# Second MLP product by Strassen's scheme, with sums of its left factor on VectorE, in a fused Mamba-2 and MLP kernel

## Chip, cores, metric

One core of a Trainium2 chip. The metric is device time of one execution in microseconds (us), median of several runs. All times are of fast runs (runs of one kernel agree within 0.8%); where a single run stands alone its state is unknown, and that is said.

## The reference

A Mamba-2 (SSD) attention block feeds an MLP with a hard-swish. All is fp32.

```python
x = attn(x, a, B, C)            # (4, 8, 768, 32) -> bridged to (3072, 256)
h = x @ w_in                    # (3072, 256) @ (256, 2048)
g = h * clip(h + 3, 0, 6) / 6
out = g @ w_out                 # (3072, 2048) @ (2048, 256)
```

## The kernel before

The tokens are worked in six blocks `k` of 512 (128 positions of four sequences). In each block TensorE first makes the 16 pieces of g (`mlp_in`, the "first product"), then the output (`mlp_out`, the "second product"). The attention steps of the next block are woven in: two of them in the first product (after pieces 9 and 13), five between parts of the second.

```python
def mlp_in(k, f):                       # piece f of 16; gT[:, f] is 128 x 512
    h = ps.tile([P, TB], FP32, name="h", tag="f")          # four buffers in PSUM, shared with "cb"
    for j in range(NK):
        nc.tensor.matmul(out=h, lhsT=w_in[:, j, f*P:(f+1)*P], rhs=yTs[k][:, j]..., ...)
    r = ffn.tile([P, TB], FP32, name="r", bufs=3)
    nc.scalar.activation(r, h, AF.Relu, bias=half, scale=1.0 / 6.0)
    nc.vector.scalar_tensor_tensor(out=gTs[k][:, f], in0=r, scalar=1.0, in1=h, op0=ALU.min, op1=ALU.mult)

def mlp_out(k, b, f0, f1):              # 128 tokens of sequence b, all 256 columns
    for f in range(f0, f1):
        nc.tensor.matmul(out=o, lhsT=gTs[k][:, f, b*P:(b+1)*P], rhs=w_out[:, f], ...)
    ...                                 # ScalarE copies o to SBUF, then a DMA

def decay(c, b):                        # GpSimd prepares the decay rows, ScalarE the exponential
    if c > 1:
        nc.gpsimd.tensor_tensor(out=L, in0=L, in1=by_j, op=ALU.add)          # L252
    nc.gpsimd.affine_select(out=L, in_=L, ...)                               # L253
    if c > 1:
        nc.scalar.activation(L, L, AF.Exp)
    ...
```

Of the kernel before, what the change touches and what calls it, by code (L numbers as in the profile page):

```python
# [1 line left out]

# [6 lines left out]
FP32 = mybir.dt.float32  # L9
# [4 lines left out]
ALU = mybir.AluOpType  # L14
# [5 lines left out]
def kernel(  # L20
# [23 lines left out]
    nc = tc.nc  # L44
    P = 128
    NB, NH, S, D = x.shape
# [4 lines left out]
    NF = DF // P  # L51
# [7 lines left out]
    const = ctx.enter_context(tc.tile_pool(name="const", bufs=1))  # L59
    loads = ctx.enter_context(tc.tile_pool(name="loads", bufs=2))  # L60
    att = ctx.enter_context(tc.tile_pool(name="att", bufs=2))
    ffn = ctx.enter_context(tc.tile_pool(name="ffn", bufs=1))
    ps = ctx.enter_context(tc.tile_pool(name="ps", bufs=4, space=PSUM))
    ps_o = ctx.enter_context(tc.tile_pool(name="ps_o", bufs=2, space=PSUM))
# [30 lines left out]
    w_out = const.tile([P, NF, DM], FP32, name="w_out")  # L95
    NP = 4
    FP = NF // NP
    NRAW = 3
    raws = {}

    def load_w(i):
# [31 lines left out]
        out=head, in_=head, pattern=[[-N * HU, 2], [-N, HU], [0, D]], compare_op=ALU.is_ge,  # L133
        fill=0.0, base=0, channel_multiplier=1)
    nc.gpsimd.affine_select(
        out=head, in_=head, pattern=[[N * HU, 2], [N, HU], [0, D]], compare_op=ALU.is_ge,
# [3 lines left out]
    def decode(i):  # L140
# [43 lines left out]
        out=a_sb, in0=a_sb, scalar1=1e-6, scalar2=1.0, op0=ALU.max, op1=ALU.min)  # L184
    nc.scalar.activation(a_sb, a_sb, AF.Ln)
    nc.vector.tensor_tensor_scan(
        out=flat, data0=run.rearrange("g c p -> g (c p)"), data1=a_sb, initial=0.0,
# [6 lines left out]
    def load_decay(c, b):  # L194
        L = big([P, NH, P], "L")
        src = cum_d[c, b * NH:(b + 1) * NH].rearrange("h p -> (h p)").unsqueeze(0)
        nc.sync.dma_start(
            out=L.rearrange("j h i -> j (h i)"), in_=src.to_broadcast([P, NH * P]))
        Ls[c, b] = L

    def load_eto(c):
        eto = att.tile([P, NB, P], FP32, name="eto")
        for h in range(NH):
            nc.sync.dma_start(  # L204
                out=eto[h * N:(h + 1) * N],
                in_=cum_d[c, h:NB * NH:NH].unsqueeze(0).to_broadcast([N, NB, P]))
        etos[c] = eto
# [19 lines left out]
    for t in range(2):  # L227
        nc.gpsimd.tensor_tensor(
            out=parity[:, t:t + 1], in0=mask[:, t, 0:1], in1=mask[:, 2 + t, 0:1], op=ALU.add)
# [17 lines left out]
    def decay(c, b):  # L247

        L = Ls[c, b]
        if c > 1:  # L250
            by_j = cum_n[:, c, b * NH:(b + 1) * NH].unsqueeze(2).to_broadcast([P, NH, P])
            nc.gpsimd.tensor_tensor(out=L, in0=L, in1=by_j, op=ALU.add)  # L252
        nc.gpsimd.affine_select(  # L253
            out=L, in_=L, pattern=[[0, NH], [1, P]], compare_op=ALU.is_ge,
            fill=-1e5, base=0, channel_multiplier=-1)
        if c > 1:
            nc.scalar.activation(L, L, AF.Exp)  # L257
        else:
            decay_exp(c, b, L, 0, NH)

    def ends(c):


        bc, xt = loaded[c]
        if c < NC - 1:
            bs = att.tile([P, NB * NH, N], FP32, name="bs")
            nc.gpsimd.tensor_tensor(  # L267
                out=bs, in0=bc[:, 1],
                in1=e_from[:, c].unsqueeze(2).to_broadcast([P, NB * NH, N]), op=ALU.mult)
            bss[c] = bs  # L270
        if c:
            eto = etos[c]
            nc.scalar.activation(eto, eto, AF.Exp)  # L273
            if c < NC - 1:
                tmp = att.tile([P, NB, P], FP32, name="tmp", bufs=1)
                nc.gpsimd.tensor_tensor(  # L276
                    out=tmp, in0=states[c - 1],
                    in1=eto[:, :, P - 1:P].to_broadcast([P, NB, P]), op=ALU.mult)
                tmps[c] = tmp

    def turn(c, p):


        bc, xt = loaded[c]
        t_ps = ps_o.tile([P, 4, P], FP32, name="t_ps", tag="o")
        for k in range(4):
            j, b = k // 2, 2 * p + k % 2
            nc.tensor.transpose(
                out=t_ps[:, k],
                in_=bc[:, j, b * NH:(b + 1) * NH].rearrange("s h n -> s (h n)"), identity=ident)  # L290
        bT = att.tile([P, 2, P], FP32, name="bT")
        nc.scalar.copy(out=bT, in_=t_ps[:, 2:4])
        cT = att.tile([P, 2, 2, P], FP32, name="cT")
        nc.vector.tensor_tensor(  # L294
            out=cT, in0=t_ps[:, 0:2].unsqueeze(2).to_broadcast([P, 2, 2, P]),
            in1=parity.unsqueeze(1).unsqueeze(3).to_broadcast([P, 2, 2, P]), op=ALU.mult)
        csT = None
        if c:
            csT = att.tile([P, 2, P], FP32, name="csT")
            nc.vector.tensor_tensor(  # L300
                out=csT, in0=t_ps[:, 0:2], in1=etos[c][:, 2 * p:2 * p + 2], op=ALU.mult)
        bTs[c, p] = bT, cT, csT

    def scores(c, b):
        bT, cT, csT = bTs[c, b // 2]
        cbs = []
        for q in range(NQ):
            rows = slice(32 * q, 32 * q + 32)
            if c == 0 and b % 2 and q < 2:
                cb = ps_o.tile([P, 2, P], FP32, name="cb", tag="o")  # L310
            else:
                cb = ps.tile([P, 2, P], FP32, name="cb", tag="f")
            nc.tensor.matmul(  # L313
                out=cb.rearrange("j h i -> j (h i)"), lhsT=bT[rows, b % 2],
                rhs=cT[rows, b % 2].rearrange("n t i -> n (t i)"), start=True, stop=True,
                tile_position=(32 * q, 0))
            cbs.append(cb)
        L = Ls[c, b]
        for q in range(NQ):
            hs = slice(2 * q, 2 * q + 2)  # L320
            nc.vector.tensor_tensor(out=L[:, hs], in0=L[:, hs], in1=cbs[q], op=ALU.mult)  # L321
# [52 lines left out]
    gTs, outs = {}, {}  # L374
# [15 lines left out]
    def mlp_out(k, b, f0, f1):  # L390
        if f0 == 0:
            outs[k, b] = ps_o.tile([P, DM], FP32, name="o", tag="o")
        o = outs[k, b]
        for f in range(f0, f1):
            nc.tensor.matmul(  # L395
                out=o, lhsT=gTs[k][:, f, b * P:(b + 1) * P], rhs=w_out[:, f],
                start=(f == 0), stop=(f == NF - 1))
        if f1 == NF:
            ob = ffn.tile([P, DM], FP32, name="ob", bufs=3)
            nc.scalar.copy(out=ob, in_=o)  # L400
            r0 = b * S + k * P
            nc.sync.dma_start(out=out[r0:r0 + P, :], in_=ob)

    def steps(c):

        ends(c)
        turn(c, 0)
        decay(c, 0)
        yield
        turn(c, 1)  # L410
        decay(c, 1)
        yield
        for b in range(NB):
            scores(c, b)
            if c + 1 < NC:
                load_decay(c + 1, b)
            if b + 2 < NB:
                decay(c, b + 2)
            if b:
                mix(c, b - 1)  # L420
            if b == 2:
                keep(c, 0)
            yield
        mix(c, 3)
        keep(c, 1)
        if 0 < c < NC - 1:
            load_eto(c + 1)

    def load(c):
        load_bc(c)  # L430
        load_x(c)
# [3 lines left out]
    def weights(i, n):  # L435
        for _ in range(n):
            next(parts[i], None)
# [7 lines left out]
    for i, _ in enumerate(steps(0)):  # L445
        if i > 3:
            weights(1, 1)
# [4 lines left out]
    for i in range(2, NP + 1):  # L452
        for j in range(4):
            weave[4 * i - 7 + j] = i
    for k in range(NC):
        todo = steps(k + 1) if k + 1 < NC else iter(())
        for f in range(NF):
            mlp_in(k, f)
            if k == 0 and f in weave:
                weights(weave[f], 1)  # L460
            if f in (9, 13):
                next(todo, None)
        if k + 2 < NC:
            load(k + 2)
        if k == 0:
            weights(NP + 1, 2)
        if k == 0:
            next(todo, None)
            for i in range(NP):
                for b in range(2):  # L470
                    mlp_out(0, b, i * FP, (i + 1) * FP)
                if i + 1 < NP:
                    weights(NP + i + 1, 2)
                    if i + 2 < NP:
                        weights(NP + i + 2, 2)
                    next(todo, None)
            mlp_out(k, 2, 0, NF)
        else:
            mlp_out(k, 0, 0, NF // 4)
            next(todo, None)  # L480
            mlp_out(k, 0, NF // 4, NF)
            next(todo, None)
            mlp_out(k, 1, 0, NF)
            next(todo, None)
            mlp_out(k, 2, 0, NF // 4)
            next(todo, None)
            mlp_out(k, 2, NF // 4, NF)
        next(todo, None)
        mlp_out(k, 3, 0, NF)


# [28 lines left out]
```

## Time and profile before

| | before |
|---|---|
| time | 432.24 us (432.01 to 432.57) |
| TensorE busy | 404.8 of 430.9 us |
| a middle block (1, 2, 3) | 65.4 us |
| of it first product with two attention steps | 28.7 us |
| of it second product with five | 36.7 us |

A block is counted from the start of its first product to the start of the next block's. TensorE is busy almost without a gap, so what counts is how long its work takes and whether it has to wait.

### The profile page before, as it was taken

To read this page: it belongs to the slowest core of one execution; us is meant where nothing else is said; L and a number is where in the kernel's file an instruction comes from. 1 tells how busy PE (TensorE), PEld (TensorE's weight loads), DVE (VectorE), ACT (ScalarE), POOL (GpSimd) and SP (SyncE) were. 2 spreads that over 40 slices of the span, in tenths; PEclk is the share of its full clock that TensorE was granted. 3 is DMA by queue.
4 is the path that set the end of the run, shared out by engine and by line. 5 is a ranking of instruction groups with operands and counts; after the bars stand their busy time and mean duration, and the time that the engine had idled before them with its cause. 6 is when DMAs were issued, how large, how long until landed. Compare 5 with 4: busy or idle time off the path is not lost.

```text
span 430.9 us, 4977 instructions
## 1 busy us (share of the span) xinstructions
PE 404.8 (94%) x1948; PEld 257.0 (60%) x1948; DVE 158.0 (37%) x289; ACT 148.9 (35%) x268; POOL 70.3 (16%) x61
## 2 busy tenths in 40 slices
PE   1579976999999999999999999999999999999996
PEld 1344432778644777644677744677744677644885
DVE  5656678960134322134322143422134421043100
ACT  5585668931145300135311134310145311134100
POOL 2500060100007500007500006825000000000000
PEclk9998988899999999999999999999999999999999
DMA  8998925911460032370023370023100000000000
GB/s 161 252 314 136 351 97 128 204 60 44 64 112 0 2 99 90 59 121 2 0 75 110 61 124 0 2 71 101 49 2 1 0 25 14 14 0 0 14 12 24
DMA packets 87607, 32.23 MB, mean 75 GB/s; under 512 B 75584, under 2 KB 81408, under 8 KB 87584
## 3 DMA queue, kind: packets, MB, share of 16 engines
q1 hardware_dynamic: 87584, 31.92, 30.4%
q8 instruction: 15, 0.25, 0.2%
q14 instruction: 8, 0.07, 0.0%
HBM read 28.67 MB, written 3.24 MB: 74 GB/s over the span
## 4 chain that ended last, share of the span: by engine, by line
PE 65%; issue 15%; SPq 6%; POOL 4%; DMA 3%; ACT 3%; DVE 2%; POOLq 0%; ACTq 0%
PE o L395 37%; PE h L381 19%; PE cb L313 3%; SPq L204 3%; PE y L342 2%; SPq L84 2%; DMA bc<-in_B_dram 2%; PE y L336 2%; POOL L L253 2%; ACT L L219 1%; DMA eto<-cum_d 1%; POOL L L252 1%; DVE gT L387 1%; PE y L348 1%; ACT r L386 1%
## 5 line engine op out<-in xcount | busy, mean ns | idle before, releaser
L381 PE MATMUL h<-yT,w_in 128*128 128x512 f32 x384 | 172.0, 603 | 6.3 <-DVE w_in L176 2.6
L395 PE MATMUL o<-w_out,gT 128*128 128x256 f32 x768 | 175.9, 387 | 0.0
L395 PEld LDWEIGHTS o<-w_out,gT 128*128 128x128 f32 x768 | 145.7, 192 | 27.0 <-issue 7.2
L381 PEld LDWEIGHTS h<-yT,w_in 128*128 128x128 f32 x384 | 72.9, 193 | 95.0 <-issue 80.3
L387 DVE SCALAR_TENSOR_TENSOR gT<-r,h 128x512 f32<-128x512 f32 x96 | 65.0, 685 | 134.4 <-ACT r L386 134.0
L386 ACT ACTIVATE r<-h,half 128x512 f32<-128x512 f32 x96 | 64.2, 686 | 70.1 <-PE h L381 70.1
L400 ACT COPY ob<-o 128x256 f32<-128x256 f32 x24 | 8.9, 373 | 162.6 <-PE o L395 129.7
L321 DVE TENSOR_TENSOR L<-L,cb 128x256 f32<-128x256 f32 x96 | 33.8, 415 | 61.3 <-PE cb L313 61.3
L276 POOL TENSOR_TENSOR tmp<-state,eto 128x512 f32<-128x512 f32 x4 | 4.2, 1048 | 173.7 <-ACT eto L273 173.7
L252 POOL TENSOR_TENSOR L<-L,cum_n 128x1024 f32<-128x1024 f32 x16 | 30.4, 1897 | 13.0 <-DMA L<-cum_d 13.0
L313 PE MATMUL cb<-cT,bT 32*128 32x256 f32 x192 | 23.2, 477 | 7.4 <-DVE cT L294 5.2
L253 POOL TENSOR_SCALAR_AFFINE_SELECT L<-L 128x1024 f32<-128x1024 f32 x24 | 27.5, 1152 | 4.4 <-DMA L<-cum_d 3.1
L219 ACT ACTIVATE L<-L,cum_n 128x128 f32<-128x128 f32 x64 | 19.3, 389 | 7.2 <-POOL L L253 7.2
L313 PEld LDWEIGHTS cb<-cT,bT 32*128 32x128 f32 x192 | 10.7, 205 | 17.6 <-DVE cT L294 6.3
L257 ACT ACTIVATE L<-L 128x1024 f32<-128x1024 f32 x16 | 17.0, 1063 | 11.8 <-POOL L L253 11.8
L366 DVE TENSOR_TENSOR state<-y,mask 128x256 f32<-128x256 f32 x10 | 4.2, 425 | 37.6 <-ACT yT L363 37.6
L342 PE MATMUL y<-L,xt 128*32 128x128 f32 x384 | 16.9, 296 | 0.1
L158 ACT ACTIVATE we<-we,bias_hi 128x1024 bf16<-128x1024 uint16 x8 | 9.2, 1148 | 11.0 <-DVE we L156 11.0
L342 PEld LDWEIGHTS y<-L,xt 128*32 128x32 f32 x384 | 9.9, 115 | 4.8 <-issue 2.1
L267 POOL TENSOR_TENSOR bs<-bc,e_from 128x512 f32<-128x512 f32 x5 | 5.9, 1188 | 38.3 <-DMA bc<-in_B_dram 30.5
L363 ACT COPY yT<-y 128x256 f32<-128x256 f32 x24 | 7.7, 373 | 10.7 <-PE y L348 9.2
L336 PEld LDWEIGHTS y<-csT,state 64*128 64x128 f32 x80 | 6.0, 184 | 6.6 <-issue 6.6
(46 smaller groups left out, 132.9 us busy)
## 6 DMA issues: line engine op xcount, KB each, us to landing
L<-cum_d SPq DMA_DIRECT2D x24, 512.0 KB, 5.0
raw<-in_moe_w_in_dram SPq DMA_DIRECT2D x4, 1024.0 KB, 8.4
raw<-in_moe_w_out_dram SPq DMA_DIRECT2D x4, 1024.0 KB, 6.5
xt<-in_x_dram SPq DMA_DIRECT2D x6, 512.0 KB, 6.9
out_dram<-ob SPq DMA_DIRECT2D x24, 128.0 KB, 1.7
bc<-in_C_dram SPq DMA_DIRECT2D x6, 256.0 KB, 5.7
bc<-in_B_dram SPq DMA_DIRECT2D x6, 256.0 KB, 7.6
eto<-cum_d SPq DMA_DIRECT2D x40, 32.0 KB, 1.9
```

Of the source, the lines that this page charges most:

```text
L219: nc.scalar.activation(Ls[c, b][:, h0 + q], src[:, q], AF.Exp, bias=cum_n[:, c, g:g + 1])
L252: nc.gpsimd.tensor_tensor(out=L, in0=L, in1=by_j, op=ALU.add)
L253: nc.gpsimd.affine_select(out=L, in_=L, pattern=[[0, NH], [1, P]], compare_op=ALU.is_ge, fill=-1e5, base=0, channel_multiplier=-1)
L257: nc.scalar.activation(L, L, AF.Exp)
L313: nc.tensor.matmul(out=cb.rearrange("j h i -> j (h i)"), lhsT=bT[rows, b % 2], rhs=cT[rows, b % 2].rearrange("n t i -> n (t i)"), start=Tr ...
L321: nc.vector.tensor_tensor(out=L[:, hs], in0=L[:, hs], in1=cbs[q], op=ALU.mult)
L336: nc.tensor.matmul(out=y_ps[u][:, k], lhsT=states[c - 1][rows, b], rhs=csT[rows, k], start=True, stop=False, skip_group_check=True)
L342: nc.tensor.matmul(out=y_ps[u][32 * q:32 * q + 32, k], lhsT=xt[:, b * NH + h], rhs=L[:, h], start=(c == 0), stop=True, tile_position=(0, 3 ...
L381: nc.tensor.matmul(out=h, lhsT=w_in[:, j, f * P:(f + 1) * P], rhs=yTs[k][:, j].rearrange("p b i -> p (b i)"), start=(j == 0), stop=(j == N ...
L386: nc.scalar.activation(r, h, AF.Relu, bias=half, scale=1.0 / 6.0)
L387: nc.vector.scalar_tensor_tensor(out=gTs[k][:, f], in0=r, scalar=1.0, in1=h, op0=ALU.min, op1=ALU.mult)
L395: nc.tensor.matmul(out=o, lhsT=gTs[k][:, f, b * P:(b + 1) * P], rhs=w_out[:, f], start=(f == 0), stop=(f == NF - 1))
```

## The change

The output of a block is a product of a 512 x 2048 by a 2048 x 256 matrix. It is cut into quarters (tokens of sequences 0, 1 and 2, 3; even and odd pieces f; left and right half of the columns). Strassen's scheme in Winograd's form makes seven products of quarters in place of eight, from sums of quarters. Four sums of the weights are made once on GpSimd; four sums of g are made in every block from 1 to 5 on VectorE, for two pairs of pieces at a time, after pieces 3, 7, 11 and 15. A "unit" is one quarter product for 128 tokens: eight matmuls over 128 columns. Its result goes to one of four slots of a PSUM tile, `oa` or `ob`, which the program calls a bank.

```diff
+    def weight_sums():                      # once, on GpSimd: t1 .. t4 from quarters of w_out
+        ...
+    def g_sums(k, j0):
+        js = slice(j0, j0 + 2)
+        a11, a12, a21, a22 = (g_quarter(k, e, r)[:, js] for r in range(2) for e in range(2))
+        s1, s2, s4 = (gsums[k][n][:, js] for n in (1, 2, 4))
+        for o, p_, q_, op in ((s1, a21, a22, ALU.add), (s2, s1, a11, ALU.subtract),
+                              (a21, a11, a21, ALU.subtract), (s4, a12, s2, ALU.subtract)):
+            nc.vector.tensor_tensor(out=o, in0=p_, in1=q_, op=op)
+    def out_units(k, t):                    # t: which 128 tokens of each pair of sequences
+        oa = ps_o.tile([P, 4, P], FP32, name="oa", tag="o")
+        unit(oa, 1, quarter(1, 0), w4[:, 1, 0]);  yield
+        unit(oa, 2, total(2), wsums[2]);          yield
+        unit(oa, 0, quarter(0, 0), w4[:, 0, 0])
+        ...                                 # x1 = oa0 (ScalarE); res0, res4 = oa1, oa2 + x1 (VectorE)
+        yield
+        ob = ps_o.tile([P, 4, P], FP32, name="ob", tag="o")
+        unit(ob, 2, total(4), w4[:, 1, 1]);       yield
+        unit(ob, 3, quarter(1, 1), wsums[4]);     yield
+        unit(ob, 0, total(1), wsums[1]);          yield
+        unit(ob, 1, quarter(0, 1), wsums[3])
+        ...                                 # three VectorE operations, two DMAs
@@ main loop
+            if k and f % 4 == 3:
+                g_sums(k, f // 2 - 1)
@@
-            mlp_out(k, 0, 0, NF // 4)
-            next(todo, None)
-            ...                             # mlp_out of 0, 1, 2, 3 with the attention steps between
+            units = itertools.chain(out_units(k, 0), out_units(k, 1))
+            for i, _ in enumerate(units):
+                if i in (0, 3, 6, 9, 11):
+                    next(todo, None)
```

The intent: TensorE is the bound, and an eighth less of the second product should shorten it, with sums on engines that have time.

More of the change, by code (lines that the diff above doesn't have):

```diff
@@ L1 @@
+import itertools
 from contextlib import ExitStack
@@ L402, in mlp_out @@
             nc.sync.dma_start(out=out[r0:r0 + P, :], in_=ob)
+    NJ = NF // 2
+    w4 = w_out.rearrange("p (j e) (m c) -> p e m j c", e=2, m=2)
+    wsums = {}
+    def weight_sums():
+        t3 = const.tile([P, NJ, P], FP32, name="t3")
+        t2, t4 = (att.tile([P, NJ, P], FP32, name=n, tag="wm") for n in ("t2", "t4"))
+        t1 = w4[:, 0, 1]
+        for o, p_, q_ in ((t3, w4[:, 1, 1], w4[:, 0, 1]), (t1, w4[:, 0, 1], w4[:, 0, 0]),
+                          (t2, w4[:, 1, 1], t1), (t4, w4[:, 1, 0], t2)):
+            nc.gpsimd.tensor_tensor(out=o, in0=p_, in1=q_, op=ALU.subtract)
+        wsums.update({1: t1, 2: t2, 3: t3, 4: t4})
@@ new lines, with g_quarter @@
+    gsums, ends_out = {}, {}
+    def g_quarter(k, e, r):
+        return gTs[k].rearrange("p (j e) (r i) -> p e r j i", e=2, r=2)[:, e, r]
+    def g_sums(k, j0):
+        if j0 == 0:
+            gsums[k] = {n: loads.tile([P, NJ, 2 * P], FP32, name=f"s{n}", tag="raw", bufs=NRAW)
+                        for n in (1, 2, 4)}
+        js = slice(j0, j0 + 2)
[4 more added lines that the diff above has]
+            nc.vector.tensor_tensor(out=o, in0=p_, in1=q_, op=op)
@@ new lines, in out_units, with quarter, total, unit @@
+    def out_units(k, t):
+        def quarter(e, r):
+            return g_quarter(k, e, r)[:, :, t * P:(t + 1) * P]
+        def total(n):
+            return gsums[k][n][:, :, t * P:(t + 1) * P]
+        def unit(bank, slot, lhs, rhs):
+            for j in range(NJ):
+                nc.tensor.matmul(
+                    out=bank[:, slot], lhsT=lhs[:, j], rhs=rhs[:, j],
+                    start=(j == 0), stop=(j == NJ - 1), skip_group_check=True)
+        oa = ps_o.tile([P, 4, P], FP32, name="oa", tag="o")
+        unit(oa, 1, quarter(1, 0), w4[:, 1, 0])
+        yield
+        unit(oa, 2, total(2), wsums[2])
+        yield
+        unit(oa, 0, quarter(0, 0), w4[:, 0, 0])
+        x1 = ffn.tile([P, P], FP32, name="x1", bufs=2)
+        nc.scalar.copy(out=x1, in_=oa[:, 0])
+        res = ffn.tile([P, 5, P], FP32, name="res", bufs=2)
+        nc.vector.tensor_tensor(
+            out=res[:, 0:5:4], in0=oa[:, 1:3], in1=x1.unsqueeze(1).to_broadcast([P, 2, P]),
+            op=ALU.add)
+        yield
+        ob = ps_o.tile([P, 4, P], FP32, name="ob", tag="o")
+        unit(ob, 2, total(4), w4[:, 1, 1])
+        yield
+        unit(ob, 3, quarter(1, 1), wsums[4])
+        yield
+        unit(ob, 0, total(1), wsums[1])
+        yield
+        unit(ob, 1, quarter(0, 1), wsums[3])
+        u = ffn.tile([P, 2, P], FP32, name="u", bufs=2)
+        nc.vector.tensor_tensor(
+            out=u, in0=ob[:, 0:2], in1=res[:, 4:5].to_broadcast([P, 2, P]), op=ALU.add)
+        nc.vector.tensor_tensor(out=res[:, 1:3], in0=ob[:, 2:4], in1=u, op=ALU.add)
+        nc.vector.tensor_tensor(out=res[:, 3], in0=ob[:, 0], in1=u[:, 1], op=ALU.add)
+        for r in range(2):
+            r0 = (t + 2 * r) * S + k * P
+            nc.sync.dma_start(
+                out=out[r0:r0 + P, :], in_=res[:, 2 * r:2 * r + 2].rearrange("p m c -> p (m c)"))
+        yield
@@ L477 @@
             mlp_out(k, 2, 0, NF)
-        else:
-            mlp_out(k, 0, 0, NF // 4)
-            next(todo, None)
-            mlp_out(k, 0, NF // 4, NF)
-            next(todo, None)
-            mlp_out(k, 1, 0, NF)
-            next(todo, None)
-            mlp_out(k, 2, 0, NF // 4)
-            next(todo, None)
-            mlp_out(k, 2, NF // 4, NF)
-        next(todo, None)
-        mlp_out(k, 3, 0, NF)
+            next(todo, None)
+            mlp_out(k, 3, 0, NF)
+            weight_sums()
+        else:
+            units = itertools.chain(out_units(k, 0), out_units(k, 1))
+            for i, _ in enumerate(units):
+                if i in (0, 3, 6, 9, 11):
+                    next(todo, None)
 _INS = ['x', 'a', 'B', 'C', 'moe_w_in', 'moe_w_out']
```

## The prediction

Statements on the hardware that no trace or run of this case shows are cut from the recorded text below, and from the expectations of x_psum and x_m64; the cuts are marked. No term of the forecast's sum is cut: it came to -16.1 + 0.8 + 18.8 + 0.6 + 5.1 = +9.2, and with the lean to the longer wait to 442.0 us. What stands behind the terms in the trace of the kernel before:

- *Pace*: the 0.109 us an instruction is that of the four transposes (0.44 us from 326.25).
- *Turns*: the view from 11.60 us shows GpSimd and VectorE side by side; "these" are its two operations. The overlap of 0.14 us is worked out from it: L165 ends at 13.75, less its own 0.685 that is 13.07, while GpSimd's operation is stamped to 13.21. The turns at 56 us are L176 from 56.18 (1.98 us, 1.22 alone) and L253 from 57.03 (2.08, 1.09 alone). L294, with its 685 ns, has 512 columns; the 0.60 is from its start at 205.04 to that of L300 at 205.64.
- *Clock*: the two stretches of the view lie around a wait of TensorE from 55.97 to 58.21. The term is an estimate: one stretch of 3.42 us at half clock, as shown there, for each of the three stalls, half of it lost.
- *Other estimates*: an addition over 128 columns at 0.3 us (425 ns for 256 columns in L366, 685 for 512 in L294); the 0.3 for blocks 4 and 5, the 0.3 for block 3 and the 0.14 of R3 are not measured.

> **What bounds the kernel now.** I read the page's busy shares and groups first, then the chain of waits, then the timelines of GpSimd and VectorE in one block. The page:
>
> ```profile
> PE 404.8 (94%) x1948; PEld 257.0 (60%) x1948; DVE 158.0 (37%) x289; ACT 148.9 (35%) x268; POOL 70.3 (16%) x61
> ...
> L395 PE MATMUL o<-w_out,gT 128*128 128x256 f32 x768 | 175.9, 387 | 0.0
> L395 PEld LDWEIGHTS o<-w_out,gT 128*128 128x128 f32 x768 | 145.7, 192 | 27.0 <-issue 7.2
> ```
>
> TensorE is the bound. The program has 384 second-product matmuls and the trace 768: each fp32 product is two instructions, each with its weight load. The chain gives their pace, in the last block and around four 128-column transposes:
>
> ```profile
> 326.25 0.44 PE t_ps L288 x4
> ...
> 372.60 27.47 PE h L381 x64
> 400.07 27.64 PE o L395 x128
> ...
> 427.78 0.37 ACT ob L400
> ```
>
> 27.47 us / 64 = 0.429 us for 512 columns, 27.64 / 128 = 0.216 for 256, 0.44 / 4 = 0.11 for 128. Pace follows the moving columns, although one weight load is stamped 192 ns. A middle block (178.2 to 243.5 us) takes 65.3 us, of which TensorE is idle some 0.1. On its way the other engines do this:
>
> ```profile
> 199.85 1.09 POOL L253 TENSOR_SCALAR_AFFINE_SELECT L<-L 128x1024 f32<-128x1024 f32 x1
> 200.92 1.90 POOL L252 TENSOR_TENSOR L<-L,cum_n 128x1024 f32<-128x1024 f32 x1
> 202.89 1.09 POOL L253 TENSOR_SCALAR_AFFINE_SELECT L<-L 128x1024 f32<-128x1024 f32 x1
> 203.95 1.90 POOL L252 TENSOR_TENSOR L<-L,cum_n 128x1024 f32<-128x1024 f32 x1
> 205.92 1.09 POOL L253 TENSOR_SCALAR_AFFINE_SELECT L<-L 128x1024 f32<-128x1024 f32 x1
> 206.99 1.90 POOL L252 TENSOR_TENSOR L<-L,cum_n 128x1024 f32<-128x1024 f32 x1
> 208.96 1.09 POOL L253 TENSOR_SCALAR_AFFINE_SELECT L<-L 128x1024 f32<-128x1024 f32 x1
> ```
> ```profile
> 202.64 2.48 DVE L387 SCALAR_TENSOR_TENSOR gT<-r,h 128x512 f32<-128x512 f32 x4 [4.53 <-ACT r L386]
> 205.04 0.68 DVE L294 TENSOR_TENSOR cT<-t_ps,parity 128x512 f32<-128x512 f32 x1
> 205.64 0.41 DVE L300 TENSOR_TENSOR csT<-t_ps,eto 128x256 f32<-128x256 f32 x1
> 206.18 0.69 DVE L387 SCALAR_TENSOR_TENSOR gT<-r,h 128x512 f32<-128x512 f32 x1
> 207.84 0.69 DVE L387 SCALAR_TENSOR_TENSOR gT<-r,h 128x512 f32<-128x512 f32 x1 [0.98 <-ACT r L386]
> ```
>
> Here GpSimd works without a pause while VectorE makes the last six pieces of g (10 to 15; the four of the first row are 10 to 13). VectorE was held until 202.64 because ScalarE stood at an exponential waiting for GpSimd. Piece 15 is ready at 208.5, just when TensorE, done with the first product at 206.92, needs it: no slack, and no loss yet.
>
> [...]
>
> ```profile
> 11.60 1.61 POOL L267 TENSOR_TENSOR bs<-bc,e_from 128x512 f32<-128x512 f32 x1 [7.79 <-ACT e_from L242]
> 12.20 1.55 DVE L165 TENSOR_TENSOR we<-we,ws 128x1024 uint16<-128x1024 uint16 x1
> ```
>
> Alone these take 1.06 and 0.685 us (medians of their groups). The preceding VectorE operation (two SBUF inputs too) held GpSimd back, then GpSimd held L165 back: they take turns, even when VectorE's next is already queued. [...] L294 of that width shows 685, consecutive independent ones start 0.60 apart. [...] the clock is the third number from the end of a row (1.00, then 0.50):
>
> ```profile
> 55.75:59.16 3.41, 1.16 (x3) 0.49 (x3) 3.41 (x4) 0.48 (x3) 3.13 (x3) 1.00 0.74 284
> 59.16:62.58 3.42, 3.42 (x5) 1.35 (x4) 1.81 (x4) 3.00 (x9) 3.42 (x3) 0.50 0.06 23
> ```
>
> **The change, part by part.** *Matmuls.* Per block 64 products over 256 columns become 2 x 7 x 8 = 112 over 128. As instructions, 128 x 0.216 = 27.6 us become 224 x 0.109 = 24.4 us: 3.2 saved, x 5 blocks = **-16.1 us**. [...] 0.12 instead of 0.109 would cost 2.5 us a block.
>
> *Sums of weights*: four GpSimd operations (about 1.9 us each by L252) after the end of block 0. They end about 6 us into block 1, whose second product starts 28 us in: hidden.
>
> *Evacuation*: per half block three VectorE operations on ob (0.42 + 0.42 + 0.3) for ScalarE's 0.37 copies. Hidden, except behind the very last matmul: **+0.8 us**.
>
> *Sums of g*: four VectorE operations of 512 columns, two SBUF inputs each, after pieces 3, 7, 11 and 15: about 2.7 us each time, 11 us a block; VectorE has 45 us free in 65. After pieces 3 and 7 GpSimd is idle and VectorE catches up within three pieces. **After piece 11 it is not.** In the frame of the block above, piece 11 ends at 203.93; until 210.05 GpSimd has four operations without a gap, and the two engines take turns. Net of the 0.14 overlap: 4 x 0.55 for VectorE and 1.76 + 0.95 + 1.76 + 0.95 for GpSimd, so the sums end at 203.95 + 7.6 = 211.6 instead of 206.6. Behind them, in order, pieces 12, 13, cT, csT, pieces 14, 15 at 0.60, 0.60, 0.60, 0.40, 0.60, then 0.69: piece 15 is ready at 215.1. TensorE finishes the first product at 206.92 as before; the first unit's matmuls alternate two instructions per odd piece, reach piece 13 at 208.2 and piece 15 at 206.92 + 14 x 0.109 = 208.45, and wait until 215.1: **6.7 us**. If VectorE gets the first turn at 203.95 (the two ask within 0.01 us of each other), one GpSimd operation fewer stands ahead: 5.8. I take 6.3. The built program's waits confirm it: the first unit waits for VectorE at exactly two of its eight products, pieces 13 and 15, and for none of the sums.
>
> The same GpSimd run lies at 132 to 145 and 262 to 278 us, so this hits blocks 1, 2 and 3: **+18.8 us**. Blocks 4 and 5 have no GpSimd work there; VectorE's own delay costs some 0.15 each: +0.3. In block 3 GpSimd goes straight on to the next chunk and may hold the sums after piece 15: +0.3.
>
> *Clock*: [...] losing half: 1.7 x 3 = **+5.1 us**.
>
> Sum: -16.1 + 0.8 + 18.8 + 0.6 + 5.1 = +9.2; as the waiting GpSimd operation at 203.95 was queued a hair earlier I lean to the longer wait: 432.3 + 9.7 = **442.0 us**.
>
> **Rivals.** *R1, no contention that matters*: [...] my alignment is off by some us. For it: the sums are short, and catching up on paper leaves 0.7 us at piece 15. Against: the turns shown at 11.6 us and again at 56 us. Then -16.1 + 0.8 + 0.8 = 418. *R2, contention but no half clock, first turn to VectorE*: 3 x 5.8 - 15 = 434 to 435. *R3, weight loads become the bound*: 128-column loads of full fp32 weights behind 128-column matmuls stand in the trace only as transposes and in half-height pairs. For it: the stamp of 192 ns[...]. At 0.14 per instruction the matmuls lose instead of gain: 31.4 a block, 477 with the stalls. Against: after a change of shape two loads of L395 start 0.11 apart.
>
> **Range and chances.** The terms of the middle are the gain (certain within 2 us), three stalls (5.5 to 7 each)[...]: 434 to 448. R1 and R3 widen the tails: 433 to 450. A result under 423.8 needs R1 (7%); over 440.9 is just below my centre (55%); between, 38%.
>
> **What would show it.** Right: units of L449 at 0.109 us an instruction, 24.4 us of such work a block; the sums (L437) at some 0.7 us in blocks 4 and 5 and after pieces 3, 7 and 15, but 1.7 to 2.6 after piece 11 in blocks 1 to 3, with L252 and L253 there stretched by some 0.5; TensorE idle about 6 us at the start of each of those second products, released by VectorE's gT (L388); a clock of 0.50 just behind; blocks 1 to 3 longer than 65.3 by 3 to 6 us, block 5 shorter by 3. Wrong: sums that run straight through, or a pace of 0.12 and more in a block without waits.

## The result, and the profile after

The change makes the kernel slower: **446.66 us** (445.9 to 446.77, 4 runs) against 432.24, a ratio of 1.033 (95% interval 1.031 to 1.035). A ratio is the mean of one kernel's fast runs over that of the other's fast runs of the same rounds, so it is not quite the ratio of the medians. Line numbers are shifted by one in the changed kernel (L387 is now L388, L252 and L253 are L253 and L254); the units are L449 and the sums of g L437.

From the page of the changed kernel: busy shares, granted clock in 40 slices (tenths of full speed), and the costliest group of the units:

```profile
PE 399.5 (90%) x2428; PEld 269.5 (61%) x2428; DVE 237.3 (53%) x409; ACT 144.0 (32%) x258; POOL 84.5 (19%) x65
...
PEclk9999987999999699999889999969999999999999
...
L449 PE MATMUL oa<-w_out,gT 128*128 128x128 f32 x320 | 42.4, 282 | 18.4 <-DVE gT L388 18.4
```

TensorE has less to do (399.5 for 404.8 us) in a longer span: it waited 18.4 us for VectorE's g, and the clock row has three dips in the middle that the kernel before does not have. In the timelines below, the first two numbers of a line are its start and its length in us, `x12` says that twelve instructions in a row are merged, and the bracket gives the engine's idle time before the line and what ended it. TensorE in block 2, at the start of the second product:

```profile
212.09 1.50 PE L449 MATMUL oa<-w_out,gT 128*128 128x128 f32 x12
218.10 0.49 PE L449 MATMUL oa<-w_out,gT 128*128 128x128 f32 x2 [4.51 <-DVE gT L388]
220.22 0.79 PE L449 MATMUL oa<-w_out,gT 128*128 128x128 f32 x2 [1.64 <-DVE gT L388]
```

The first twelve instructions run; those that need piece 13 wait 4.51 us, those that need piece 15 another 1.64. VectorE in the same stretch (after the two pieces 10 and 11, the four sums, then pieces 12, 13, cT, csT and pieces 14, 15):

```profile
207.81 1.28 DVE L388 SCALAR_TENSOR_TENSOR gT<-r,h 128x512 f32<-128x512 f32 x2 [4.30 <-ACT r L387]
209.12 2.43 DVE L437 TENSOR_TENSOR s<-gT 128x512 f32<-128x512 f32 x1
211.59 1.46 DVE L437 TENSOR_TENSOR s<-s,gT 128x512 f32<-128x512 f32 x1
212.98 2.38 DVE L437 TENSOR_TENSOR gT<-gT 128x512 f32<-128x512 f32 x1
215.28 1.57 DVE L437 TENSOR_TENSOR s<-gT,s 128x512 f32<-128x512 f32 x1
216.77 1.27 DVE L388 SCALAR_TENSOR_TENSOR gT<-r,h 128x512 f32<-128x512 f32 x2
```

and GpSimd:

```profile
209.12 1.90 POOL L253 TENSOR_TENSOR L<-L,cum_n 128x1024 f32<-128x1024 f32 x1
211.09 1.43 POOL L254 TENSOR_SCALAR_AFFINE_SELECT L<-L 128x1024 f32<-128x1024 f32 x1
212.49 2.32 POOL L253 TENSOR_TENSOR L<-L,cum_n 128x1024 f32<-128x1024 f32 x1
214.88 1.43 POOL L254 TENSOR_SCALAR_AFFINE_SELECT L<-L 128x1024 f32<-128x1024 f32 x1
```

Read the two side by side. The first sum is stamped from 209.12 but ends only at 211.55, some 0.5 us after GpSimd's 1.90 us operation (to 211.02); the next GpSimd operation takes 1.43 in place of 1.09, and so on, turn by turn. The four sums take 7.7 us (209.12 to 216.85); away from GpSimd they have a median of 0.68 to 0.69 us each. Last, two stretches of block 2 with the granted clock as third number from the end (before it the busy times of TensorE, its weight loads, VectorE, ScalarE, GpSimd; behind it the DMA share and GB/s):

```profile
210.00:218.48 8.48, 3.97 (x20) 2.50 (x18) 8.45 (x7) 2.24 (x4) 7.62 (x5) 1.00 0.00 0
218.48:225.30 6.82, 5.18 (x26) 4.20 (x26) 5.60 (x12) 0.70 (x1) 0.00 (x0) 0.50 0.01 2
```

The half clock begins while TensorE waits and lasts until 225.30, 5.1 us after the wait is over.

How long the blocks took in each trace, from the start of the first product to the next block's (for block 5: its second product, which no attention step interrupts, from the start of its first instruction to the start of its last):

| run | block 1 | block 2 | block 3 | block 4 | block 5, second product |
|---|---|---|---|---|---|
| before | 65.4 | 65.4 | 65.4 | 63.5 | 27.4 |
| changed | 71.8 | 71.7 | 71.7 | 61.1 | 25.1 |
| x_sums | 74.1 | 74.6 | 74.8 | 63.5 | 27.4 |
| x_nosums | 64.8 | 62.9 | 62.9 | 61.1 | 25.1 |
| x_psum | 64.2 | 64.2 | 65.8 | 61.1 | 25.1 |
| x_fill | 69.4 | 69.4 | 70.5 | 61.1 | 25.1 |
| x_late | 64.4 | 64.4 | 65.9 | 61.7 | 26.5 |
| y_late | 64.2 | 64.2 | 64.7 | 62.4 | 27.7 |
| y_late_noload | 64.2 | 64.2 | 64.2 | 62.4 | 27.7 |
| y_bank | 62.9 | 62.9 | 63.9 | 61.1 | 25.1 |

So the change gains 2.4 us in block 4 and 2.3 in block 5, and loses 6.4 in each of blocks 1 to 3. Block 0, whose code is the same in all, took 78.1 to 80.8 us: an offset of up to some 2.7 us between single traces that the edits do not explain. Part of it is the clock: the two shortest (x_fill, y_late) are the two whose traces have 3.4 us at half clock in block 0, the others have some 10. So effects of a few us are read from the blocks, not from the totals.

### The profile page after: what moved, and what is told of

It is laid out like the page before. It is cut to its first block, busy times and chain, and to the rows that moved or that the text cites. A ratio compares the mean times of both kernels' runs of the same rounds, so it can differ in the third digit from the quotient of the medians.

```text
span 445.0 us, 6046 instructions
## 1 busy us (share of the span) xinstructions
PE 399.5 (90%) x2428; PEld 269.5 (61%) x2428; DVE 237.3 (53%) x409; ACT 144.0 (32%) x258; POOL 84.5 (19%) x65
## 4 chain that ended last, share of the span: by engine, by line
PE 57%; issue 17%; DVE 11%; SPq 4%; POOL 4%; ACT 3%; DMA 2%; POOLq 0%; DVEq 0%; ACTq 0%
PE ob L449 15%; PE h L382 13%; PE oa L449 13%; PE o L396 7%; DVE s L437 4%; PE cb L314 4%; DVE gT L388 3%; PE y L343 3%; SPq L85 2%; DMA bc<-in_B_dram 2%; PE y L337 2%; DVE gT L437 2%; POOL L L254 1%; ACT L L220 1%; PE y L349 1%
## 5 line engine op out<-in xcount | busy, mean ns | idle before, releaser
L388 DVE SCALAR_TENSOR_TENSOR gT<-r,h 128x512 f32<-128x512 f32 x96 | 63.8, 683 | 65.5 <-ACT r L387 65.4
L387 ACT ACTIVATE r<-h,half 128x512 f32<-128x512 f32 x96 | 64.2, 686 | 99.1 <-PE h L382 80.3
L449 PE MATMUL oa<-w_out,gT 128*128 128x128 f32 x320 | 42.4, 282 | 18.4 <-DVE gT L388 18.4
L449 PEld LDWEIGHTS oa<-w_out,gT 128*128 128x128 f32 x320 | 38.9, 194 | 23.0 <-DVE gT L388 19.6
L449 PE MATMUL ob<-w_out,s 128*128 128x128 f32 x320 | 39.8, 278 | 0.0
L449 PE MATMUL ob<-t,gT 128*128 128x128 f32 x320 | 39.4, 276 | 0.0
L449 PEld LDWEIGHTS ob<-w_out,s 128*128 128x128 f32 x320 | 37.3, 192 | 1.4 <-issue 1.4
L449 PEld LDWEIGHTS ob<-t,gT 128*128 128x128 f32 x320 | 37.3, 192 | 0.7 <-issue 0.7
L253 POOL TENSOR_TENSOR L<-L,cum_n 128x1024 f32<-128x1024 f32 x16 | 32.0, 2003 | 19.6 <-DMA L<-cum_d 19.6
L396 PE MATMUL o<-w_out,gT 128*128 128x256 f32 x128 | 31.7, 409 | 0.0
L254 POOL TENSOR_SCALAR_AFFINE_SELECT L<-L 128x1024 f32<-128x1024 f32 x24 | 29.9, 1249 | 5.0 <-DMA L<-cum_d 3.9
L396 PEld LDWEIGHTS o<-w_out,gT 128*128 128x128 f32 x128 | 25.9, 206 | 5.2 <-issue 1.0
L449 PEld LDWEIGHTS oa<-t,s 128*128 128x128 f32 x160 | 23.2, 231 | 2.3 <-issue 2.3
L449 PE MATMUL oa<-t,s 128*128 128x128 f32 x160 | 24.5, 317 | 0.0
```

What stands on the lines that cost most here:

```text
L254: nc.gpsimd.affine_select(out=L, in_=L, pattern=[[0, NH], [1, P]], compare_op=ALU.is_ge, fill=-1e5, base=0, channel_multiplier=-1)
L396: nc.tensor.matmul(out=o, lhsT=gTs[k][:, f, b * P:(b + 1) * P], rhs=w_out[:, f], start=(f == 0), stop=(f == NF - 1))
L449: nc.tensor.matmul(out=bank[:, slot], lhsT=lhs[:, j], rhs=rhs[:, j], start=(j == 0), stop=(j == NJ - 1), skip_group_check=True)
```

## The experiments

The theory to be tested: the sums after piece 11 meet GpSimd's run, the two engines take turns because a sum has two SBUF operands, pieces 12 to 15 come late, TensorE waits, and the wait lowers its clock. The rivals: VectorE simply has too much in its queue; the clock plays no part; the half-width matmuls are themselves the loss. All the runs below were made on one chip, where the kernel before took 431.3 to 431.6 us (median).

### x_nosums: the seven half products without their sums

```diff
-            gsums[k] = {n: loads.tile(...) for n in (1, 2, 4)}
+            gsums[k] = gsums.get(k - 1) or {n: loads.tile(...) for n in (1, 2, 4)}
+        if j0 or k > 1:
+            return
+        for n in (1, 2, 4):
+            nc.vector.memset(gsums[k][n], 1.0)
+        return                    # the sums are never made; wrong result on purpose
```

> The changed kernel without the sums of g (the three sum tiles are set once and never computed; a wrong result on purpose). It shows what seven half products are worth without their sums. Theory: no wait over 0.3 us at the first unit and no half clock from block 1 on; the second product takes 224 x 0.112 = 25.0 us in place of 27.6, so 432.3 - 5 x 2.6 + 0.8 = 420 us (419 to 422). Rival (the half-width matmuls themselves are the loss, by weight loads): 440 us or more.

Measured: 422.17 us (ratio 0.979, 0.977 to 0.981). TensorE has no wait over 0.1 us at the start of a second product. Blocks 2 to 4 save 2.4 us each; block 1 saves less, because the three memsets stand in VectorE's queue there (a wait of 1.60 us in the first product that the edit itself brought). That artefact is most of the 2 us over the estimate. The half-width matmuls are a gain, so the rival that blames them falls.

### x_sums: the sums without the seven half products

```diff
 # the kernel before, plus:
+            if k and f % 4 == 3:
+                g_sums(k, f // 2 - 1)
 # in g_sums the third sum goes to a scratch place, so the result stays right:
-                              (a21, a11, a21, ALU.subtract), (s4, a12, s2, ALU.subtract)):
+                              (s4, a11, a21, ALU.subtract), (s4, a12, s2, ALU.subtract)):
```

> The kernel before with the sums of g added at the same four places and never used (result unchanged; the third sum goes to a scratch tile). Theory: the sums alone bring the whole loss. TensorE goes through its first eight instructions of the second product and then waits at the scores for the banks of pieces 12 to 15 until piece 15 is done, some 6.4 us, in blocks 1 to 3, and runs at half clock for some 5 us behind it: 432.3 + 3 x (6.4 + 2.6) = 459 us (455 to 461). With x_nosums the two effects add up to the change: 459 + 420 - 432 = 447. Rival (the loss needs the new order of the units): within 2 us of 432.

Measured: 459.37 us (ratio 1.066, 1.063 to 1.069), result correct. TensorE's timeline in block 2:

```profile
213.87 1.89 PE L395 MATMUL o<-w_out,gT 128*128 128x256 f32 x8
219.29 1.81 PE L313 MATMUL cb<-cT,bT 32*128 32x256 f32 x4 [3.52 <-DVE gT L387]
```

The first eight instructions of the old second product run, then the attention scores wait for the PSUM buffers of late pieces. The sums alone cost 27.8 us, in blocks 1 to 3 and nowhere else. The expectation had the time right (459) but not its parts: in block 2 TensorE was idle for 3.52 + 0.31 us, not 6.4, and ran at half clock for 10.24 us (217.78 to 228.02), not some 5. That the total came out is luck. With x_nosums, 459.4 + 422.2 - 431.6 = 450.0 (448 without the memset wait), 447 with the change: the two effects nearly add up, although the loss is split differently in the two kernels.

### x_psum: the same sums with one operand in PSUM

```diff
+            if j0 == 4 and k < NC - 1:      # the sums after piece 11, blocks 1 to 4
+                q_ = y_pss[k][0].rearrange("p (j i) c -> p j (i c)", j=2)    # a PSUM tile
             nc.vector.tensor_tensor(out=o, in0=p_, in1=q_, op=op)
```

> The changed kernel, but in blocks 1 to 4 the four sums after piece 11 take their second operand from PSUM instead of SBUF (a wrong result on purpose; same count, order and width of VectorE operations). Theory[...]: GpSimd's L253 and L254 in that stretch go back to 1.90 and 1.09 us, the four sums take some 2.6 us together instead of 7.6, piece 15 is ready some 5 us earlier, TensorE waits at most 1.7 us in place of 6.7 in blocks 1 to 3 and the half-clock stretch behind it goes or shrinks: 446.7 - 3 x (5 to 7.5) = 424 to 432 us. Rival (VectorE simply has too much in its queue): same durations per operation as in the changed kernel's free stretches, so the wait stays near 6.7 us and the time stays within 2 us of 446.

Measured: 425.52 us (ratio 0.986, 0.984 to 0.988; the result is wrong). Two of the four sums on VectorE, then two GpSimd operations in the same stretch, then TensorE at piece 15:

```profile
201.49 0.68 DVE L439 TENSOR_TENSOR s<-gT,y 128x512 f32<-128x512 f32 x1
202.21 0.69 DVE L439 TENSOR_TENSOR s<-s,y 128x512 f32<-128x512 f32 x1
```
```profile
201.60 1.90 POOL L253 TENSOR_TENSOR L<-L,cum_n 128x1024 f32<-128x1024 f32 x1
203.56 1.09 POOL L254 TENSOR_SCALAR_AFFINE_SELECT L<-L 128x1024 f32<-128x1024 f32 x1
```
```profile
207.47 0.49 PE L451 MATMUL oa<-w_out,gT 128*128 128x128 f32 x2 [1.17 <-DVE gT L388]
```

VectorE has as many operations of the same width in the same order, side by side with the same GpSimd run, and both engines are at full speed. This is the run that decides: the loss comes from the second SBUF operand, not from the length of VectorE's queue. What the queue costs by itself is the remaining wait of 1.17 us, and no half clock followed it.

### x_fill: TensorE kept busy while it waits

```diff
+    FILL = {6: 20, 7: 8}
             for j in range(NJ):
+                if fill and 0 < k < NC - 2 and j > 5:        # first unit of blocks 1 to 3
+                    for q in range(FILL[j]):
+                        nc.tensor.matmul(out=bank[:, 3], lhsT=lhs[:, q % 4], rhs=rhs[:, q % 4],
+                                         start=False, stop=False, skip_group_check=True)
```

> The changed kernel with 28 filler products (56 instructions of about 0.112 us, 6.2 us in all, into an unused part of the bank; result unchanged) inside the wait of the first unit in blocks 1 to 3, so that TensorE is busy while it would wait. Theory (idle TensorE lowers the clock, and the half clock behind the wait costs 2.6 us a block): the wait for piece 15 ends at the same time, no clock of 0.50 behind it, blocks 1 to 3 take 71.7 - 2.6 = 69.1 us, total 446.7 - 7.8 = 439 us. Rival (the clock plays no part, only the wait counts): 446 to 448 us.

Measured: 440.08 us (ratio 1.021, 1.018 to 1.024), result correct. The clock of a stretch in the middle of what was the wait, full of filler:

```profile
210.24:213.65 3.41, 3.41 (x33) 3.41 (x33) 3.41 (x3) 0.00 (x0) 3.34 (x3) 1.00 0.00 0
```

The half clock is gone from blocks 1 to 3, and each of blocks 1 and 2 is 2.3 to 2.4 us shorter, although TensorE does 6.2 us more work in them. Block 3 is shorter by only 1.2, because at full speed a later unit waits there 0.84 us for a sum. By the blocks, then, 6 us of the loss were the clock (2.4 + 2.3 + 1.2). The rest is the wait itself: a block of x_fill is still 6.5 us longer than one of x_nosums (69.4 and 62.9).

### x_late, y_late, y_late_noload: the sums where GpSimd is done

If the theory holds, the sums of pieces 8 to 15 should stand behind piece 15, and there are three units that need no sum (quarters 1,0, 0,0 and 1,1) to fill the time. x_late moves the sums alone:

```diff
-            if k and f % 4 == 3:
+            if k and f in (3, 7):
                 g_sums(k, f // 2 - 1)
+            if k and f == 15:
+                g_sums(k, 4, 4)        # four operations of 1024 columns
```

> The changed kernel with only the sums of pieces 8 to 15 moved behind piece 15; units and scores in the changed kernel's order. Theory: the first unit no longer waits, but the second unit needs the second sum, which takes two turns with GpSimd first: a wait of some 2 us in blocks 1 to 3 and 0.5 in 4 and 5, perhaps with a short half clock: 425 to 432 us. This tells what the place of the sums is worth without the order of the units. Rival (the total of VectorE work is what counts, not its place): 446 us.

Measured: 428.34 us (ratio 0.993, 0.991 to 0.995). Moving two calls wins 18 us back. The time is as expected. The wait at the second unit was 1.2 us in blocks 1 to 3, 0.3 in block 4 and 1.1 in block 5, block 3 had one more of 1.0 at a later unit, and no half clock followed.

y_late also puts the units without sums first, the attention steps after units 2, 5, 7, 9 and 11, and the unit with the shortest addition behind it last; and it loads the next decay rows later (meant for block 3); y_late_noload is the same without that:

```diff
-                if i in (0, 3, 6, 9, 11):
+                if i in (2, 5, 7, 9, 11):
+        # order of units: oa1, oa0, ob3, oa2, ob0, ob1, then u, res2, res3; ob2 last, then res1
-                load_decay(c + 1, b)
+                for q in (b,) if c < 2 else range(NB) if b == 2 else ():
+                    load_decay(c + 1, q)
```

> The changed kernel with the sums of pieces 8 to 15 made in one go after piece 15 (four operations of 1024 columns), the three units that need no sum first, the scores after the third unit, the last unit one that needs a single short addition behind it, and the loads of the next chunk's decay rows moved to the second half of a block so that GpSimd is not kept busy in block 3. Theory: piece 15 is ready at its old time, GpSimd has only two operations left to take turns with, the second sum is done before the fourth unit reaches it, so no wait over 0.3 us and no half clock: each of blocks 1 to 5 saves the 2.4 us that the run without sums showed, 432 - 12 = 420 us (418 to 423), faster than both. Rival (the sums cost TensorE time wherever they stand): 435 us or more.

> The same as y_late but with the loads of the decay rows where they were. Theory: only block 3 differs; there GpSimd goes on to the rows of the last chunk and takes turns with all four of the late sums, so the fourth unit waits some 2 to 4 us in that block alone: 422 to 426 us. If GpSimd's work there does not matter: the same as y_late within 0.5 us.

Measured: y_late 426.94 us (ratio 0.990, 0.987 to 0.994), y_late_noload 427.79 (0.991, 0.988 to 0.995). Both expectations missed. The loads make no clear difference: in y_late_noload block 3 is as long as blocks 1 and 2, so that idea was wrong at this order of units. And both are some 5 us slower than the kernel without sums (422.17). The trace of y_late shows why, on TensorE and on VectorE at the end of block 2:

```profile
233.51 2.05 PE L449 MATMUL ob<-t,gT 128*128 128x128 f32 x16
236.60 2.05 PE L449 MATMUL ob<-w_out,s 128*128 128x128 f32 x16 [1.04 <-DVE res L482]
```
```profile
236.26 0.28 DVE L482 TENSOR_TENSOR res<-ob,u 128x128 f32<-128x128 f32 x1
```

The last unit (slot 2 of bank ob) waits 1.04 us until VectorE has read slots 0, 1 and 3 of the same bank. The sum it uses was ready long before (at 211.2). The wait goes by the bank: TensorE goes on at 236.60, just after VectorE's last read of it (L482, 236.26 to 236.54), and in y_bank below, where the last unit writes another bank or stands earlier, the wait is gone. Whether the unit could write its own slot while VectorE reads the others was not shown: no run here goes without the wait.

### y_bank: the last unit in the other bank

Against y_late_noload:

```diff
+        if t == 0:
+            unit(ob, 2, total(4), w4[:, 1, 1]);  yield      # before ob0 and ob1
         unit(ob, 0, total(1), wsums[1]);  yield
         unit(ob, 1, quarter(0, 1), wsums[3])
         ...                                                # u, res2, res3
-        unit(ob, 2, total(4), w4[:, 1, 1])
+        if t == 1:
+            yield
+            unit(oa, 3, total(4), w4[:, 1, 1])              # a free slot of bank oa
```

> The kernel with the late sums (loads of the decay rows where they were), with one thing mended: its trace showed TensorE idle for 1.04 us before the last unit of every second half block, because that unit writes the bank from which VectorE is just then reading. In the second half the last unit now goes to the free slot of the other bank; in the first half it stands two units earlier. Theory: that wait goes in all five blocks (twice in block 5): 427 - 6 x 1.04 = 421 us (419 to 423), and the result stays correct. If the wait came from the sum it reads (ready long before by the trace), it stays: 426 to 428 us.

Measured: **420.44 us** (418.71 to 421.19; ratio 0.974, 0.971 to 0.976), correct. This beats both kernels: the kernel before by 2.6%, the changed one by 26 us. Two blocks of it in the view by stretches:

```profile
112.35:175.27 62.92, 62.84 (x425) 43.18 (x424) 33.99 (x61) 17.60 (x30) 23.69 (x14) 1.00 0.28 62
238.19:302.12 63.93, 63.11 (x427) 43.27 (x426) 36.02 (x62) 17.23 (x29) 28.39 (x17) 1.00 0.29 62
```

TensorE idles 0.1 us in block 1, the clock is full, and the length equals that of the run without any sums (block 2 of x_nosums, 62.9): the sums of g cost nothing there. Against y_late_noload (64.2) each wait of 1.04 us cost a block 1.3: the ends of matmuls in a trace are modelled, so the idle time shown is a little less than what a wait costs (in y_late the weight loads waited 7.9 us in six such waits, 1.3 each). Block 3 still waits 0.74 us at one unit, where GpSimd goes straight on to the last block's rows.

### x_m64: why 0.112 and not 0.109

```diff
+                M = P // 2 if k == NC - 1 and j else P
                 nc.tensor.matmul(
-                    out=bank[:, slot], lhsT=lhs[:, j], rhs=rhs[:, j],
+                    out=bank[:M, slot], lhsT=lhs[:, j, :M], rhs=rhs[:, j],
```

> The changed kernel, but in block 5 all products of a unit except the first load only 64 of their 128 weight columns (a wrong result on purpose, the moving side is still 128 columns). It asks why the pace is 0.112 us an instruction and not the 0.109 of the transposes. Theory (the weight load[...] adds the difference): 0.109 us for these instructions, block 5's second product 24.5 us in place of 25.1. Rival (the pace is that of 128 moving columns in fp32 with accumulation): 0.112 as before.

Measured, one run of unknown state with a wrong result on purpose: consecutive instructions with 64 weight columns start 0.109 us apart (with 128 columns, in the changed kernel, 0.111 to 0.112). The weight loads with 64 columns, with their mean length in ns as the number after the busy time:

```profile
L450 PEld LDWEIGHTS ob<-t,gT 128*64 128x64 f32 x56 | 6.0, 137 | 0.5
```

A load stamped 137 ns goes with the pace of 0.109, one of 192 ns (128 columns, the units of the changed kernel) with 0.112. The transposes fit this: their loads of 128 columns, one to a transpose, are stamped 141 ns. So the last 0.0025 us of the pace points to the weight load. With 64 weight columns the output is halved to 64 partitions too, and no run separates the two; the transposes, which fill 128 partitions at 0.109, speak against the output. The forecast for the block missed: its second product took 29.0 us, not 24.5, because around each change between 128 and 64 columns the distances are 0.16 to 0.21 us.

## Why the prediction was right, by its steps

- *TensorE is the bound and the loss is a wait of its own*: right. The two waits and what ended them (L388) are those forecast, at the two instructions named.
- *Turns of VectorE and GpSimd*: right; x_psum shows that the second SBUF operand brings them (0.68 to 0.69 us a sum with one operand in PSUM, 1.46 to 2.43 with both in SBUF). Forecast: sums from 203.95 to 211.6, so 7.6 us, with GpSimd first; measured 7.7, GpSimd first.
- *Size of the wait*: TensorE was to go on 215.1 - 178.2 = 36.9 us after the start of the block; in block 2 of the changed kernel it went on at 220.22 - 183.38 = 36.84. As idle time 4.51 + 1.64 = 6.15 us for the 6.3 taken; x_fill against x_nosums puts the cost at 6.5.
- *Which blocks*: right, 1 to 3 only. The extra 0.3 for block 3 did not show (71.7 as in block 2), nor the 0.3 for blocks 4 and 5 (block 4 took 61.1 us with and without the sums).
- *Gain of the matmuls*: mis-sized. The term was 3.2 us a block, from 0.109 an instruction; x_nosums measured 2.4, 12 us in all for 16, and so outside the "certain within 2 us". The pace was 0.112, and x_m64 points to the weight load for 0.0025 of it: the step took the transposes' pace, with loads stamped 141 ns, for that of products of 128 weight columns, with loads stamped 192, as rival R3 had warned in a stronger form.
- *Half clock*: right in kind, mis-sized: 1.7 us a block taken, 2.3 measured by x_fill. In block 2 it lasted 5.1 us behind the wait, for the 3.4 taken. All three blocks had 6.83 us at half clock, from 146.80, 218.48 and 290.16. These starts lie 71.68 us apart, 21 times 3.413 us, and in the clock records of both kernels' traces each stretch between two changes of the clock lasts a whole number of 3.413 us (3.41, 6.83, 10.24 and so on, up to 351.57). So the three blocks are hardly three independent cases. In x_m64, whose code is the same there, the same blocks took 71.0 to 71.5.
- *Tail*: forecast 0.8. Behind the last matmul VectorE's three operations run from 440.82 to 441.91, where ScalarE's copy took 0.37: 0.7 more.

With the measured terms: 432.2 - 12.1 + 3 x 6.15 + 3 x 2.3 + 0.7 = 446.2, measured 446.7; the forecast of 442.0 was low by the gain (4 us) and the clock (2 us), of which the terms that did not show (0.6, and 0.5 for the longer wait) give back one. R1 and R2 are refuted by the timelines and by x_fill; R3 in the strong form (0.14) by x_nosums.

## What to carry to other kernels

Before giving work to an idle VectorE, look at what GpSimd does in the same microseconds: with two SBUF operands each sum here waited out a whole GpSimd operation, so the cost was GpSimd's durations, not VectorE's own (7.7 us for four sums of 0.69). Place such work where GpSimd is done, or give it a PSUM operand, and let TensorE begin with the parts that do not need it: here the same arithmetic gave 446.7 us in one place and 420.4 in another. And price a wait of TensorE of this length with the half clock behind it, which here added over a third of the wait once more (2.3 us on 6.2).

## What the traces show of the hardware

- *VectorE and GpSimd*: with two SBUF operands in each sum, four sums of 0.69 us took 7.7 us between four GpSimd operations, although each sum is stamped to start within 0.04 us of the end of the one before (changed kernel, 209.12 to 216.85). The first sum ended at 211.55, which is 0.53 us after GpSimd's stamped end at 211.02, some 0.16 less than a sum takes alone.
- *Clock*: a stretch of 3.41 us in which TensorE was busy 1.16 us was followed by half clock (before, 55.75 to 59.16), while one with the wait of 1.17 us in x_psum (busy 2.24 of 3.41, 205.02 to 208.43) was not. No threshold comes out of these traces: in x_late a stretch with 2.58 us busy (70.08 to 73.49) was followed by half clock too. The half clock lasted 3.41, 6.83 or, in x_sums, 10.24 us.
- *Pace in fp32*: 0.216 and 0.429 us an instruction for 256 and 512 moving columns, two instructions a product; for 128 columns 0.112 with weight loads stamped 192 ns, and 0.109 with the shorter loads of the transposes (141 ns) and of x_m64 (137 ns).
- *Change of shape*: from 128 to 64 weight columns and back, starts are 0.16 to 0.21 us apart around each change (x_m64).
